# P V of the third last group ahead of the score sums of the last group, and the last V pieces issued then

## The chip, the cores and the metric

The kernel runs on one core of one Trainium2 chip. The time is device microseconds of one execution; lower is better. Each comparison takes executions of the kernel before on the same chip in the same rounds. "Group", "piece" and "span" below are meant as follows: the kernel works in 64 groups (0 to 63); the last group's V is loaded in 7 pieces; the span is the time from the first to the last instruction in a profile, about 1.8 us less than the execution's time. "P V" is the product of the exponentials of the scores (P) with V. TensorE is "warm" where its granted clock is 1.00 and "cold" where it is 0.50. Times inside a profile are microseconds from the start of its span.

## The reference, cut to what matters

```python
q = (x @ wq).reshape(B, Sq, H, Dh)                      # B=8, Sq=1, H=32, Dh=128
scores = einsum("bhqd,bhkd->bhqk", q, k_cache) * Dh**-0.5   # Sk=4096
p = softmax(scores)
o = einsum("bhqk,bhkd->bhqd", p, v_cache)
a = o.reshape(B, Sq, H * Dh) @ wo
# ... b = a small MLP of x; result g * a + (1 - g) * b
```

K and V are 512 MiB together in bf16 and each element is used once, so reading them is nearly all of the work. The MLP runs in the shadow of the loads and does not matter here.

## The kernel before

A group is four heads of one batch row: 4 MB of K and 4 MB of V. There are two K buffers and two V buffers; group g uses buffer g % 2. For each group VectorE multiplies K by q in four chunks, TensorE adds the products up in 8 matmuls per chunk ("score sum" of the chunk), VectorE reduces the rest, and after the fourth chunk comes the softmax. P V of a group is done one group later, on TensorE, in the stream of the next group's score sums.

```python
def load_v_pieces(g):                       # only for the last group, 63
    s = g % 2
    ...
        t = load("sync", dst, part, f"sVl{n}", [v_done.get(g - 2)])   # buffer is free after P V of 61

def scores(g, between):                     # mult: VectorE product and TensorE sum of a chunk
    mult(g, 0); between(0)
    mult(g, 1); between(1)
    for c in range(NCK):                    # NCK = 4
        reduce(g, c)
        if c + 2 < NCK:
            mult(g, c + 2); between(c + 2)

def between(c, g=g):
    ...
    if c == 2:
        ...
        if g == NG - 1:                     # NG - 1 = 63, NG - 3 = 61
            pv(NG - 3, 0, 1)
            evict(NG - 3)
            load_v_pieces(g)
    if c == 3:
        if 1 <= g < NG - 2:
            pv(g - 1, 0, 1)                 # the other groups: behind sum 3
            evict(g - 1)
        ...
```

K of groups 62 and 63, V of 61 and V of 62 are all issued before the last V pieces. After the last group's scores follow P V of 62, the exponentials of 63, "turned" P V of 63 (128 small matmuls, each needing its V piece), the output projection and the store. Instructions are emitted per engine in program order; in the timelines below the matmuls run in that order.

Of the kernel before, what the change touches and what calls it, by code (L numbers as in the profile page):

```python
# [23 lines left out]
NG = NHG * B  # L24
# [11 lines left out]
class Stream:  # L36
# [8 lines left out]
    def op(self, engine, fn, waits=(), dma=None):  # L45

        rec = [fn, [w for w in waits if w is not None], None, dma]
        self.ops[engine].append(rec)
        if dma is not None:
            return ("dma", *dma)  # L50
        return ("op", engine, rec)
# [33 lines left out]
def bass_gated_mix__mha_block_cached__mixer_channel_mlp__decode_kernel(  # L85
# [20 lines left out]
    def pstride(t):  # L106
        return t[tuple([slice(None)] * len(t.shape))].ap[0][0]
# [78 lines left out]
    def load(engine, dst, src, name, waits=()):  # L186
        return op(engine, lambda e: e.dma_start(dst, src), waits, dma=(nc.alloc_semaphore(name), 16))  # L187
# [24 lines left out]
    def kv_src(cache, g):  # L212
        hg, b = divmod(g, B)
        return cache[b, hg * HB:(hg + 1) * HB].rearrange("h (p t) d -> (h p) t d", p=32)
# [4 lines left out]
    def load_k(g):  # L219
        s = g % 2  # L220
        nK[s] += 1
        src = kv_src(A_k_cache, g)
        k_land[g] = op("sync", lambda e: e.dma_start(KB[s][:, :, :], src), [k_done.get(g - 2)], dma=(sK[s], 16 * nK[s]))

    def load_v(g):
        s = g % 2
        nV[s] += 1
        src = kv_src(A_v_cache, g)
        t = op("sync", lambda e: e.dma_start(VB[s][:, :, :], src), [v_done.get(g - 2)], dma=(sV[s], 16 * nV[s]))
        v_land[g] = [(t, 0, NTT)]  # L230
# [3 lines left out]
    def load_v_pieces(g):  # L234
        s = g % 2
        src = kv_src(A_v_cache, g)
        v_land[g] = []
        t0 = 0
        for n, nt in enumerate(V_LAST):
            dst, part = VB[s][:, t0:t0 + nt, :], src[:, t0:t0 + nt, :]  # L240
            t = load("sync", dst, part, f"sVl{n}", [v_done.get(g - 2)])
            v_land[g].append((t, t0, t0 + nt))
            t0 += nt
        assert t0 == NTT
# [140 lines left out]
    def softmax(g):  # L385
        s = g % 2
        t = op("vector", lambda e: e.tensor_reduce(out=mA[:, 0:1], in_=s_sb[:, s, :], axis=AX.X, op=ALU.max),  # L387
               [v_red[g, NCK - 1], c_mA])
        t = op("vector", lambda e: e.transpose(mB[:, :], mA[:, :]), [t])  # L389
        t = op("vector", lambda e: e.tensor_reduce(out=gm[:, :], in_=mB[:, :], axis=AX.X, op=ALU.max), [t])  # L390
        gmb = bass.AP(tensor=gm, offset=0, ap=[[pstride(gm), 128], [0, 32]])
        t = op("vector", lambda e: e.tensor_scalar(out=mC[:, :], in0=gmb, scalar1=-1.0, scalar2=None, op0=ALU.mult), [t])
        v_nm[g] = op("vector", lambda e: e.transpose(mD[:, s, :], mC[:, :]), [t, a_exp.get(g - 2)])  # L393
        for h in range(HB):
            q = slice(32 * h, 32 * h + 32)
            a_exp[g] = op("scalar", lambda e, h=h, q=q: e.activation(  # L396
                out=P[q, s, :, h], in_=s_sb[q, s, :], func=ACT.Exp, bias=mD[q, s, 0:1], scale=1.0),
                [v_nm[g], p_pv.get(g - 2), v_rs.get(g - 2), c_P])

    def rowsum(g):  # L400
        s = g % 2
        v_rs[g] = op("vector", lambda e: e.tensor_reduce(  # L402
            out=rs[:, s, :], in_=P[:, s, :, :].rearrange("p t h -> p h t"), axis=AX.X, op=ALU.add),
            [a_exp[g], p_z.get(g - 2)])

    def pv(g, part, parts):
        s = g % 2
        for land, t0, t1 in v_land[g]:
            t0, t1 = max(t0, part * NTT // parts), min(t1, (part + 1) * NTT // parts)
            for tq in range(t0 // TQ, t1 // TQ):  # L410
                j = tq % 4
                o = o_ps[s][32 * j:32 * j + TQ * HB, :]
                w = [land, a_exp[g], a_ev.get(g - 2), *c_ps] if tq == t0 // TQ else ()
                p_pv[g] = op("tensor", lambda e, o=o, tq=tq: e.matmul(  # L414
                    o, lhsT=P[:, s, tq * TQ:(tq + 1) * TQ, :].rearrange("p t h -> p (t h)"),
                    rhs=VB[s][:, tq * TQ:(tq + 1) * TQ, :].rearrange("p t d -> p (t d)"),
                    start=(tq < 4), stop=(tq >= NTQ - 4)), w)
        v_done[g] = p_pv[g]

    def total(g):  # L420
        p_z[g] = op("tensor", lambda e: e.matmul(  # L421
            oz_ps[:, HB:2 * HB], lhsT=ones[:, :], rhs=rs[:, g % 2, :], start=True, stop=True),
            [v_rs[g], v_norm.get(g - 1), c_ones])

    def evict(g):
        s = g % 2
        a_ev[g] = op("scalar", lambda e: e.activation(out=O_sb[:].rearrange("p t d -> p (t d)"), in_=o_ps[s][:, :],  # L427
                                                      func=ACT.Copy), [p_pv[g], p_oz.get(g - 1)])

    def gather(g):  # L430
        for tt in range(TQ):
            p_oz[g] = op("tensor", lambda e, tt=tt: e.matmul(  # L432
                oz_ps[:, 0:HB], lhsT=O_sb[:, tt, :], rhs=sel16[:, tt, :], start=(tt == 0), stop=(tt == TQ - 1)),
                [a_ev[g], v_norm.get(g - 1), c_sel16] if tt == 0 else ())

    def norm(g):
        hg, b = divmod(g, B)
        t = op("vector", lambda e: e.reciprocal(out=rz[:, :], in_=oz_ps[:, HB:2 * HB]), [p_oz[g]])  # L438
        v_norm[g] = op("vector", lambda e: e.tensor_tensor(  # L439
            out=OT_sb[:, hg * HB:(hg + 1) * HB, b], in0=oz_ps[:, 0:HB], in1=rz[:, :], op=ALU.mult), [t])  # L440
# [4 lines left out]
    def up_proj(j0, j1):  # L445
        for jt in range(j0, j1):
            for kt in range(NKF + 2):
                o, n, at = up_ps[:, jt * B:(jt + 1) * B], 128, kt * F + jt
                if kt >= NKF:
                    o, n, at = up_ps[64 * (kt - NKF):64 * (kt - NKF) + 64, jt * B:(jt + 1) * B], 64, NKF * F + jt  # L450
                w = bass.AP(tensor=RB, offset=at, ap=[[pstride(RB), 128], [NJ, n]])
                st["p_up"] = op("tensor", lambda e, w=w, o=o, kt=kt: e.matmul(  # L452
                    o, lhsT=w, rhs=yT_sb[:, kt, :], start=(kt == 0), stop=(kt >= NKF)),
                    [*ld_w1, v_yT] if jt == kt == 0 else ())
# [27 lines left out]
    def down_proj(j0, j1):  # L482
        for jt in range(j0, j1):
            st["p_down"] = quarters(hT_sb[:, jt, :], w2_sb[:, jt, :], jt == 0, jt == NJ - 1,
                                    [st["ld_w2"], st["v_h"], c_yps] if jt == 0 else ())
# [41 lines left out]
    for g in range(NG):  # L527
        if 1 <= g <= NG - 3:
            load_k(g + 1)
        if 1 <= g <= NG - 2 and g != NG - 3:  # L530
            load_v(g)

        def between(c, g=g):
            if c == 0 and 2 <= g < NG - 1:
                gather(g - 2)
            if c == 1 and g >= 1:
                rowsum(g - 1)
                if g < NG - 1:
                    if g >= 2:
                        norm(g - 2)  # L540
                    total(g - 1)
            if c == 2:
                if UP0 <= g < UP0 + UPN:
                    up_proj((g - UP0) * NJ // UPN, (g - UP0 + 1) * NJ // UPN)
                if DN0 <= g < DN0 + DNN:
                    down_proj((g - DN0) * NJ // DNN, (g - DN0 + 1) * NJ // DNN)
                if g >= AP0 and done_a[0] * B + B + 1 <= g:
                    a_proj(done_a[0])
                    done_a[0] += 1
                if g == NG - 1:  # L550
                    pv(NG - 3, 0, 1)
                    evict(NG - 3)
                    load_v_pieces(g)
            if c == 3:
                if 1 <= g < NG - 2:
                    pv(g - 1, 0, 1)
                    evict(g - 1)
                if g == NG - 1:
                    gather(NG - 3)
                if g == UP0 + UPN:  # L560
                    act_h()
                if g == DN0 + DNN:
                    b_out()

        scores(g, between)
        if g == NG - 3:
            load_k(g + 2)
            load_v(g)
        if g + 1 < NG:
            q_of(g + 1)  # L570
        if g == UP0 + UPN:
            load_w2()
        if g == DN0 + DNN:
            load_wo()
        softmax(g)
    last = NG - 1
    norm(last - 2)
    pv(last - 1, 0, 1)
# [54 lines left out]
```

## Time and profile before

| | kernel before |
|---|---|
| time, median (3 executions) | 1313.88 us (1313.2 to 1313.92) |
| span of the profile | 1313.1 us |
| mean load rate | 425 GB/s |
| last V pieces issued from | 1295.41 us |
| last piece landed | 1309.0 us |
| last reduce of group 63 | 1297.24 us |

The load stream bounds the kernel over almost the whole span. From the page of the kernel before: DMA is the busy share, in tenths, of 40 slices of the span; the line under it is what they moved in GB/s.

```profile
DMA  9999999999999999999999999999999999999996
GB/s 400 417 431 434 432 432 429 430 432 433 429 434 431 432 428 430 422 420 431 432 432 431 431 432 430 431 431 432 431 431 431 431 431 430 431 432 429 431 411 268
```

Only the last slices fall off. Among the waits of SyncE, which issues the loads, is this one (who waited, for what; us in total, times, longest):

```profile
SPq L187 <- PE psb L414: 32.7, 1, 32.7
```

L187 is the issue of the V pieces, L414 is P V. Most of such a wait costs nothing, because earlier loads keep the DMA busy. The windows view, one microsecond each (busy shares of TensorE, its weight loads, VectorE, ScalarE, GpSimd; granted clock; DMA share; GB/s), shows what this wait costs the stream:

```profile
1289.00:1290.00 1.00, 1.00 (x4) 0.32 (x3) 1.00 (x2) 0.00 (x0) 0.00 (x0) 0.50 0.23 98
...
1292.00:1293.00 1.00, 1.00 (x7) 0.45 (x5) 1.00 (x2) 0.00 (x0) 0.00 (x0) 1.00 0.16 66
1293.00:1294.00 1.00, 1.00 (x15) 0.35 (x17) 1.00 (x1) 0.00 (x0) 0.00 (x0) 1.00 0.00 0
1294.00:1295.00 1.00, 1.00 (x28) 0.40 (x16) 0.97 (x2) 0.00 (x0) 0.00 (x0) 1.00 0.00 0
1295.00:1296.00 1.00, 1.00 (x12) 0.35 (x5) 0.00 (x0) 0.58 (x1) 0.00 (x0) 1.00 0.00 0
1296.00:1297.00 1.00, 1.00 (x6) 0.53 (x5) 0.00 (x0) 0.01 (x1) 0.00 (x0) 1.00 0.85 147
```

The queue has nothing left and stands idle until the pieces are issued. A packet counts in the window in which it starts; by the packets of the trace no data move from 1294.13 to 1296.37. The stream also thins out ahead of that, to 98 GB/s in the microsecond from 1289. The timeline of TensorE, VectorE and SyncE in that stretch (start, duration, engine, line, operation, count, idle time before and its releaser):

```profile
1285.05 6.31 PE L364 MATMUL psb<-p,ident 128*128 128x512 bf16 x16 [4.16 <-DVE p L354]
1288.68 0.69 DVE L369 TENSOR_REDUCE s_sb<-psb 128x32 f32<-128x512 f32 x1 [0.89 <-PE psb L364]
1291.63 1.90 PE L364 MATMUL psb<-p,ident 128*128 128x512 bf16 x8 [0.27 <-DVE p L354]
1293.46 1.90 PE L414 MATMUL psb<-VB,P 128*16 128x512 bf16 x32
1295.30 1.90 PE L364 MATMUL psb<-p,ident 128*128 128x512 bf16 x8
1295.41 3.46 SPq L187 DMA_DIRECT2D VB<-in_A_v_cache_dram  x7
1297.24 0.69 DVE L369 TENSOR_REDUCE s_sb<-psb 128x32 f32<-128x512 f32 x1 [2.26 <-PE psb L364]
...
1307.75 1.02 PE L508 MATMUL psb<-P,VB 128*128 128x4 bf16 x24 [2.01 <-DMA VB<-in_A_v_cache_dram]
1309.03 0.37 PE L508 MATMUL psb<-P,VB 128*128 128x4 bf16 x8 [0.25 <-DMA VB<-in_A_v_cache_dram]
```

L364 with x8 is one score sum. P V of group 61 runs at 1293.46, the pieces go out when it is done, and the last turned matmuls (L508) wait for them 2 us and more. Yet V of group 61 had landed at 1284.5 (issued at 1258.92, 25.6 us to landing in the view of the DMA issues).

One more thing to see: the 16 matmuls that start at 1285.05 take 6.31 us, while later ones take 1.90 us for 8. The page's clock line and the windows view give the reason: the granted TensorE clock was 0.50 from 1283.7 to 1290.5 (the first of the windows above shows it).

### The profile page before, as it was taken

How to read it: one execution, taken by the hardware profiler on the slowest of the kernel's cores; microseconds unless marked ns; L12 is line 12 of the kernel's file. 1: busy time of each engine (PE TensorE's matmuls, PEld its weight loads, DVE VectorE, ACT ScalarE, POOL GpSimd, SP SyncE). 2: the span in 40 equal slices, each digit the busy share in tenths (PEclk: the TensorE clock that was granted, in tenths of full speed). 3: DMA queues.
4: the chain of work that ended last, by engine and by line, in shares of the span. 5: the costliest groups of instructions: out<-in, count | busy, mean ns of one | idle time of the engine just before them, and what ended most of it. 6: DMA issues, size and time to landing. Idle time of an engine off the chain costs nothing.

```text
span 1313.1 us, 12641 instructions
## 1 busy us (share of the span) xinstructions
PE 877.7 (67%) x5428; PEld 419.8 (32%) x5428; DVE 871.2 (66%) x1061; ACT 204.1 (16%) x393; POOL 2.5 (0%) x13
## 2 busy tenths in 40 slices
PE   3466877676638676646766755766676776676686
PEld 1133433343313333222332322333232333232233
DVE  4576676676747676646667676676676676776665
ACT  1201011111110110101111111111111111101101
POOL 0000000000000000000000000000000000000000
PEclk8878777968777888778868888777868777878877
DMA  9999999999999999999999999999999999999996
GB/s 400 417 431 434 432 432 429 430 432 433 429 434 431 432 428 430 422 420 431 432 432 431 431 432 430 431 431 432 431 431 431 431 431 430 431 432 429 431 411 268
DMA packets 25255, 557.77 MB, mean 425 GB/s; under 512 B 2528, under 2 KB 6640, under 8 KB 7536
## 3 DMA queue, kind: packets, MB, share of 16 engines
q1 hardware_dynamic: 24944, 556.95, 99.0%
q8 instruction: 42, 0.69, 0.2%
q14 instruction: 13, 0.11, 0.0%
q10 hardware_dynamic: 256, 0.03, 0.0%
HBM read 556.96 MB, written 0.01 MB: 424 GB/s over the span
## 4 chain that ended last, share of the span: by engine, by line
DMA 65%; DVE 18%; PE 16%; ACT 0%; issue 0%; SPq 0%
DMA KB<-in_A_k_cache_dram 64%; DVE p L354 14%; PE psb L364 13%; PE psb L432 3%; DVE s_sb L369 3%; DMA VB<-in_A_v_cache_dram 1%; PE psb L414 0%; SPq L187 0%; DVE rz L438 0%; DVE OT_sb L439 0%; ACT P L396 0%; ACT L467 0%; ACT O_sb L427 0%; PE psb L477 0%; DVE mA L387 0%
## 5 line engine op out<-in xcount | busy, mean ns | idle before, releaser
L364 PE MATMUL psb<-p,ident 128*128 128x512 bf16 x2048 | 645.5, 473 | 413.9 <-DVE p L354 413.9
L354 DVE TENSOR_TENSOR p<-KB,q_bc 128x4096 bf16<-128x4096 bf16 x256 | 579.5, 2285 | 181.7 <-DMA KB<-in_A_k_cache_dram 178.6
L364 PEld LDWEIGHTS psb<-p,ident 128*128 128x128 bf16 x2048 | 225.2, 120 | 725.2 <-DVE p L354 447.7
L369 DVE TENSOR_REDUCE s_sb<-psb 128x32 f32<-128x512 f32 x256 | 175.6, 686 | 103.9 <-PE psb L364 103.7
L427 ACT ACTIVATE O_sb<-psb 128x512 f32<-128x512 f32 x63 | 37.6, 597 | 1037.9 <-PE psb L414 1037.9
L396 ACT ACTIVATE P<-s_sb,mD 32x128 bf16<-32x128 f32 x256 | 147.0, 574 | 10.6 <-DVE mD L393 6.7
L414 PE MATMUL psb<-VB,P 128*16 128x512 bf16 x2016 | 119.9, 379 | 0.0
L432 PEld LDWEIGHTS psb<-sel,O_sb 128*128 128x128 f32 x504 | 101.9, 280 | 21.3 <-issue 16.3
L438 DVE RECIPROCAL rz<-psb 128x4 f32<-128x4 f32 x63 | 11.5, 182 | 125.6 <-PE psb L432 125.6
L432 PE MATMUL psb<-sel,O_sb 128*128 128x4 f32 x504 | 88.2, 298 | 0.0
L414 PEld LDWEIGHTS psb<-VB,P 128*16 128x16 bf16 x2016 | 44.7, 89 | 69.9 <-issue 26.3
L402 DVE TENSOR_REDUCE rs<-P 128x4 f32<-128x512 bf16 x64 | 43.5, 679 | 2.1 <-ACT P L396 2.1
L421 PEld LDWEIGHTS psb<-rs,ones 128*128 128x128 f32 x128 | 31.3, 246 | 15.8 <-issue 8.6
L348 ACT ACTIVATE q_bc<-psb 128x128 bf16<-128x128 f32 x64 | 17.4, 271 | 32.4 <-PE psb L346 32.4
L421 PE MATMUL psb<-rs,ones 128*128 128x4 f32 x128 | 21.2, 236 | 0.0
L452 PEld LDWEIGHTS psb<-yT_sb,RB 128*128 128x128 bf16 (+1 forms) x216 | 19.4, 165 | 3.4
L452 PE MATMUL psb<-yT_sb,RB 128*128 128x8 bf16 (+1 forms) x216 | 19.8, 227 | 0.0
L387 DVE TENSOR_REDUCE mA<-s_sb 128x1 f32<-128x128 f32 x64 | 18.3, 286 | 2.2
L389 DVE STREAM_TRANSPOSE mB<-mA 128x32 f32<-128x32 f32 x64 | 13.6, 213 | 2.2
L393 DVE STREAM_TRANSPOSE mD<-mC 128x32 f32<-128x32 f32 x64 | 13.6, 212 | 2.2
L346 PEld LDWEIGHTS psb<-Q,Sel 128*128 128x128 bf16 x64 | 6.1, 96 | 27.4 <-issue 27.2
L346 PE MATMUL psb<-Q,Sel 128*128 128x128 bf16 x64 | 14.7, 230 | 0.0
(63 smaller groups left out, 86.5 us busy)
## 6 DMA issues: line engine op xcount, KB each, us to landing
KB<-in_A_k_cache_dram SPq DMA_DIRECT2D x64, 4096.0 KB, 26.0
VB<-in_A_v_cache_dram SPq DMA_DIRECT2D x63, 4096.0 KB, 31.8
RB<-in_B_w_dram SPq DMA_DIRECT2D x1, 5184.0 KB, 43.8
RB<-in_B_w_dram SPq DMA_DIRECT2D x1, 4608.0 KB, 35.8
RB<-in_A_wo_dram SPq DMA_DIRECT2D x1, 4608.0 KB, 43.9
RB<-in_A_wq_dram SPq DMA_DIRECT2D x1, 4096.0 KB, 12.6
VB<-in_A_v_cache_dram SPq DMA_DIRECT2D x2, 1024.0 KB, 5.7
VB<-in_A_v_cache_dram SPq DMA_DIRECT2D x3, 512.0 KB, 8.4
```

Source lines behind the costliest of these rows:

```text
L346: t = op("tensor", lambda e: e.matmul(qb_ps[:, 0:DH], lhsT=Sel[:, b, :], rhs=Q4[:, hg * DH:(hg + 1) * DH], start=True, stop=True), [a_Q[hg ...
L354: v_mult[g, c] = op("vector", lambda e: e.tensor_tensor(out=p1[:, par, :, :], in0=KB[s][:, c * CT:(c + 1) * CT, :], in1=qb, op=ALU.mult), ...
L364: p_sum[g, c] = op("tensor", lambda e, r=r, n=n: e.matmul(tr_ps[par][:, :], lhsT=ident[:, :], rhs=r, start=(n == 0), stop=(n == NCH - 1)), w)
L369: v_red[g, c] = op("vector", lambda e: e.tensor_reduce(out=s_sb[:, s, c * CT:(c + 1) * CT], in_=tr_ps[par][:, :].rearrange("p (t c) -> p t ...
L387: t = op("vector", lambda e: e.tensor_reduce(out=mA[:, 0:1], in_=s_sb[:, s, :], axis=AX.X, op=ALU.max), [v_red[g, NCK - 1], c_mA])
L396: a_exp[g] = op("scalar", lambda e, h=h, q=q: e.activation(out=P[q, s, :, h], in_=s_sb[q, s, :], func=ACT.Exp, bias=mD[q, s, 0:1], scale=1.0),
L402: v_rs[g] = op("vector", lambda e: e.tensor_reduce(out=rs[:, s, :], in_=P[:, s, :, :].rearrange("p t h -> p h t"), axis=AX.X, op=ALU.add), ...
L414: p_pv[g] = op("tensor", lambda e, o=o, tq=tq: e.matmul(o, lhsT=P[:, s, tq * TQ:(tq + 1) * TQ, :].rearrange("p t h -> p (t h)"), rhs=VB[s] ...
L421: p_z[g] = op("tensor", lambda e: e.matmul(oz_ps[:, HB:2 * HB], lhsT=ones[:, :], rhs=rs[:, g % 2, :], start=True, stop=True), [v_rs[g], v_ ...
L427: a_ev[g] = op("scalar", lambda e: e.activation(out=O_sb[:].rearrange("p t d -> p (t d)"), in_=o_ps[s][:, :], func=ACT.Copy), [p_pv[g], p_ ...
L432: p_oz[g] = op("tensor", lambda e, tt=tt: e.matmul(oz_ps[:, 0:HB], lhsT=O_sb[:, tt, :], rhs=sel16[:, tt, :], start=(tt == 0), stop=(tt == ...
L452: st["p_up"] = op("tensor", lambda e, w=w, o=o, kt=kt: e.matmul(o, lhsT=w, rhs=yT_sb[:, kt, :], start=(kt == 0), stop=(kt >= NKF)), [*ld_w ...
```

## The change

P V of group 61 moves ahead of all score sums of group 63, so that the buffer is free and the last V pieces are issued as soon as V of 61 is there. Nothing else changes. The order of the other engines' instructions stays as it was; only TensorE's order changes.

```diff
                     done_a[0] += 1
-                if g == NG - 1:
-                    pv(NG - 3, 0, 1)
-                    evict(NG - 3)
-                    load_v_pieces(g)
             if c == 3:
@@
         softmax(g)
+        if g == NG - 2:
+            pv(g - 1, 0, 1)
+            evict(g - 1)
+            load_v_pieces(g + 1)
     last = NG - 1
```

## The prediction

> **What bounds the kernel now.** Over the span it is the load stream: 425 GB/s mean, 99% of the queue's time (page, parts 2 and 3). The change touches only the last 30 us. There the SyncE waits and the timeline show one hole: the last V pieces (group 63) are issued at 1295.4 us, after a 32.7 us wait for P V of group 61, although V of group 62 landed at 1294.6 (issue 1262.4 + 32.2). One-microsecond windows show 66, 0, 0, 0, 147 GB/s from 1292 to 1297. The last piece lands at 1309.0, and the chain of waits ends with it; norm, output projection and store follow to 1313.1.
>
> P V of group 61 could run earlier: its V lands at 1284.5 (issue 1258.92 + 25.6). It stands behind the score sums of chunks 0 to 2 of group 63, which wait for VectorE's products.
>
> **What the change moves.** Nothing is added or removed; 32 P V matmuls go from between chunk sums 2 and 3 to ahead of chunk sum 0. TensorE will wait for V of group 61 (1284.5), run P V, and release the pieces at about 1287.5 to 1288.2, 7 us sooner. The hole closes; the last piece should land at about 1304.5 (estimate: 1294.6 plus 4 MB at 430 GB/s, 9.8 us).
>
> **What that costs.** The score sums of group 63 become the limit. Today chunk sum 0 starts at 1285.05. With P V ahead it starts near 1288, because TensorE runs at half clock there: it idled from 1280.9, and the granted clock is 0.50 from 1283.7 to 1290.5. A chunk sum takes 3.6 us cold and 1.90 warm; P V takes 1.90 warm, so I estimate 3.6 cold. The clock changes only at steps of 3.413 us, and rose only after a step with at least 2.68 us of score or P V matmuls (never after 2.60). The Trainium skill, "TensorE: Matmul & The Clock Gate", Part 1, states this free-running window; the trace agrees. So cold time after 1284.5 is 2.7 to 6.1 us by the phase, and chunk sum 0 ends at 1289.7 to 1291.4 (now 1288.66). Reduce, product, reduce, product, last sum take another 7.65 us: the last reduce starts at 1297.3 to 1299.1. Today it starts at 1297.24, of which 0.9 us is P V ahead of the last chunk sum; that comes back. Net delay of the softmax 0.1 to 1.8 us, mean about 1.
>
> **Sum.** Without DMA waits the tail now would run turned P V from 1301.7 to 1305.74 (with gather, total), then 32 more matmuls, 1.1 us: 1306.9. With the delay: 1307.0 to 1308.7, against 1309.4 now. Of 5 us earlier data, 0.7 to 2.4 us reach the end.
>
> **Prediction:** 1312.5 us (before 1313.88), range 1311.3 to 1314.0. Chances: faster by over 2% 0.005, within 2% 0.99, slower by over 2% 0.005.
>
> **What would show it.** Pieces issued near 1288; no empty windows around 1294; last piece landed before 1305.5; P V of 61 starts near 1284.5 at clock 0.50 and takes over 3 us; first reduce of group 63 starts 1 to 2.8 us after 1288.68, the last 0 to 1.8 us after 1297.24; the last turned P V matmuls wait for no DMA.
>
> **What would make it wrong.** P V may not count as activity for the clock (16 of 128 columns): then the sums stay cold, the delay is near 3 us and the change loses 0.5 us. V of 61 or the pieces may land later than estimated.

## More of the kernel before

The profiled execution took 1314.88 us.

## The result, and the profile after

| | before | changed |
|---|---|---|
| time, median (4 executions each) | 1313.9 us (1313.2 to 1314.78) | 1312.42 us (1311.7 to 1314.29) |
| span of the profile | 1313.1 us | 1310.0 us |
| last V pieces issued from | 1295.41 us | 1287.68 us |
| last piece landed | 1309.0 us | 1304.4 us |
| first / last reduce of group 63 | 1288.68 / 1297.24 us | 1289.50 / 1297.18 us |

The ratio is 0.9991, 95% interval 0.9973 to 1.0008: not even certainly faster in this first comparison. Ratios in this text are the mean time of one kernel's fast runs over that of the other's in the same rounds, so not quite the ratio of the medians quoted.

The changed kernel ran in three later calls too, five executions each, on three different chips. Of all 19 executions the median is 1311.9 us (1310.14 to 1314.29); of the 31 of the kernel before that ran beside them it is 1313.6 us (1312.66 to 1314.87). The medians differ by 1.7 us. The changed kernel spreads over 4.2 us, the kernel before over 2.2 us; the spread has to be explained as well as the gain.

The page of the changed kernel, the same two lines; the last slice moves 295 GB/s instead of 268:

```profile
DMA  9999999999999999999999999999999999999997
GB/s 401 418 432 431 432 431 431 432 432 432 432 429 431 430 430 432 425 417 432 432 431 432 430 432 431 432 430 432 431 429 431 430 432 431 431 432 432 431 418 295
```

The wait of SyncE after the change:

```profile
SPq L187 <- PE psb L414: 26.5, 1, 26.5
```

The same stretch in the windows view after the change, with two earlier lines; the stream no longer stops, though it still thins out where V of 62 ends (180 GB/s in the microsecond from 1289):

```profile
1285.00:1286.00 1.00, 1.00 (x16) 0.34 (x12) 1.00 (x2) 0.00 (x0) 0.00 (x0) 0.50 1.06 459
...
1289.00:1290.00 1.00, 1.00 (x7) 0.45 (x5) 0.50 (x1) 0.00 (x0) 0.00 (x0) 1.00 0.62 180
...
1292.00:1293.00 1.00, 0.55 (x3) 0.31 (x4) 1.00 (x3) 0.00 (x0) 0.00 (x0) 1.00 0.75 311
1293.00:1294.00 1.00, 1.00 (x7) 0.39 (x4) 1.00 (x1) 0.00 (x0) 0.00 (x0) 1.00 0.94 385
1294.00:1295.00 1.00, 0.35 (x2) 0.00 (x0) 1.00 (x1) 0.00 (x0) 0.00 (x0) 1.00 0.97 410
1295.00:1296.00 1.00, 0.76 (x4) 0.40 (x5) 0.79 (x2) 0.00 (x0) 0.00 (x0) 1.00 1.01 393
```

And the timeline:

```profile
1284.28 3.35 PE L414 MATMUL psb<-VB,P 128*16 128x512 bf16 x32 [4.93 <-DMA VB<-in_A_v_cache_dram]
1287.56 3.63 PE L364 MATMUL psb<-p,ident 128*128 128x512 bf16 x16
1287.68 4.04 SPq L187 DMA_DIRECT2D VB<-in_A_v_cache_dram  x7
1289.50 0.69 DVE L369 TENSOR_REDUCE s_sb<-psb 128x32 f32<-128x512 f32 x1 [3.25 <-PE psb L364]
...
1297.18 0.69 DVE L369 TENSOR_REDUCE s_sb<-psb 128x32 f32<-128x512 f32 x1 [1.40 <-PE psb L364]
...
1304.44 1.85 PE L508 MATMUL psb<-P,VB 128*128 128x4 bf16 x64
```

P V now waits for the landing of V of 61 and starts at 1284.28. It takes 3.35 us instead of 1.90, because the clock is at 0.50 from 1283.83 to 1287.25. The pieces go out 7.7 us sooner. At the end the 64 last turned matmuls run in one stretch and wait for no load. The chain of waits (start, duration, what) has changed its nature; before it ended with a load,

```profile
1298.43 10.55 DMA VB<-in_A_v_cache_dram
1309.03 0.39 PE psb L508 x8
```

and now its last load is V of group 61, and compute follows from there to the end:

```profile
1257.41 26.83 DMA VB<-in_A_v_cache_dram
1284.24 0.04 issue
1284.28 3.35 PE psb L414 x32
1287.63 1.85 PE psb L364 x8
1289.47 0.02 issue
1289.50 0.69 DVE s_sb L369
...
1304.58 1.72 PE psb L508 x64
```

So 7.7 us of earlier issue became 4.6 us of earlier landing (the queue had to finish V of 62 first, and its own end is slow: 219 and 195 GB/s in the two microseconds from 1301), and of these 3.1 us reached the end of this profile (1313.1 to 1310.0). This compares a slow execution of the kernel before (1314.88 us) with a fast one of the changed kernel (1311.82 us); the medians of all executions differ by 1.7 us.

### The profile page after: what moved, and what is told of

The parts are those of the page before. It is cut to its first block, busy times and chain, and to the rows that moved or that the text cites. A ratio compares the mean times of both kernels' runs of the same rounds, so it can differ in the third digit from the quotient of the medians.

```text
span 1310.0 us, 12641 instructions
## 1 busy us (share of the span) xinstructions
PE 870.3 (66%) x5428; PEld 416.0 (32%) x5428; DVE 870.8 (66%) x1061; ACT 204.1 (16%) x393; POOL 2.5 (0%) x13
## 4 chain that ended last, share of the span: by engine, by line
DMA 66%; DVE 17%; PE 16%; issue 0%; ACT 0%; SPq 0%
DMA KB<-in_A_k_cache_dram 64%; DVE p L354 14%; PE psb L364 12%; PE psb L432 3%; DVE s_sb L369 3%; DMA VB<-in_A_v_cache_dram 2%; PE psb L414 0%; PE psb L508 0%; DVE rz L438 0%; DVE OT_sb L439 0%; ACT P L396 0%; ACT L467 0%; SPq L187 0%; SPq L223 0%; PE psb L477 0%
## 5 line engine op out<-in xcount | busy, mean ns | idle before, releaser
L364 PE MATMUL psb<-p,ident 128*128 128x512 bf16 x2048 | 638.9, 469 | 415.7 <-DVE p L354 415.7
L432 PEld LDWEIGHTS psb<-sel,O_sb 128*128 128x128 f32 x504 | 99.7, 274 | 21.0 <-issue 16.2
L432 PE MATMUL psb<-sel,O_sb 128*128 128x4 f32 x504 | 86.3, 294 | 0.0
```

The source lines that it names most:

```text
L364: p_sum[g, c] = op("tensor", lambda e, r=r, n=n: e.matmul(tr_ps[par][:, :], lhsT=ident[:, :], rhs=r, start=(n == 0), stop=(n == NCH - 1)), w)
L432: p_oz[g] = op("tensor", lambda e, tt=tt: e.matmul(oz_ps[:, 0:HB], lhsT=O_sb[:, tt, :], rhs=sel16[:, tt, :], start=(tt == 0), stop=(tt == ...
```

## The experiments

Theory: two limits end this kernel. One is the landing of the last piece, set by when the pieces are issued. The other is the chain of score sums, softmax and turned P V of group 63, which P V of 61 now heads. The first limit moved away; the second decides, and its length depends on whether TensorE's clock is at half rate there. The clock changes only at steps of 3.413 us whose phase differs between executions, which gives the spread. Rivals: the moved 1.9 us on TensorE bring the gain, not the loads; or the spread comes from the landing of V of 61, not from the clock.

All eleven runs gave correct results. "chip 10" and so on are names of chips; times are compared within one call.

### First call (chip 10): the kernel before 1313.99 us, 9 executions, 1313.18 to 1314.87

**The changed kernel again.** No edit.

> The changed kernel again, unaltered, for a second look at its spread. Theory (the clock's phase decides whether P V of group 61 and the first score sum of group 63 run cold): executions spread over about 1311.5 to 1314.5 us, median near 1312.5; if the profiled one is a slow one, the granted clock stays 0.50 until 6 us after P V starts and the first reduce of group 63 comes about 1.8 us later than in the trace at hand (1289.5). Rival (V of group 61 lands at different times, the clock does not matter): in a slow trace P V starts over 1 us later than 1284.3, with the first chunk sum at 1.9 us.

Measured: 1311.54 us (1310.14 to 1313.96), ratio 0.9982 (0.9969 to 0.9994). The traced execution was the fastest one, with a span of 1308.3 us. Its timeline, to be read beside that of the first profile of the changed kernel:

```profile
1283.89 1.90 PE L414 MATMUL psb<-VB,P 128*16 128x512 bf16 x32 [3.65 <-DMA VB<-in_A_v_cache_dram]
1285.73 3.63 PE L364 MATMUL psb<-p,ident 128*128 128x512 bf16 x16
1287.66 0.69 DVE L369 TENSOR_REDUCE s_sb<-psb 128x32 f32<-128x512 f32 x1 [0.53 <-PE psb L364]
```

P V started only 0.4 us sooner than in the first profile, but at full clock: it took 1.90 us, and the first reduce came 1.8 us sooner. The prediction had taken it for granted that the clock is low there. It is not always: the 3.413 us step of the clock from 1281.96 on held 1.48 us of P V, and the clock did not fall after it. Two of the five executions (1310.14 and 1310.38) lie below the 1311.5 that was expected.

**Only the order.** TensorE's order as changed; the pieces wait also for VectorE's last product, so that they are issued as late as before.

```diff
-            t = load("sync", dst, part, f"sVl{n}", [v_done.get(g - 2)])
+            t = load("sync", dst, part, f"sVl{n}", [v_done.get(g - 2), hold])
@@ c == 3, g == NG - 1
+                    load_v_pieces(g, v_mult[g, 3])
@@ after softmax(NG - 2)
-            load_v_pieces(g + 1)
```

> TensorE's order as in the changed kernel, but the last V pieces also wait for VectorE's last product of group 63 (about 1295.2 us), so they are issued about when the kernel before issued them. Theory (the earlier issue brings the gain, the earlier P V alone only costs): last piece lands near 1309, the last turned P V waits for it, time 1313.3 to 1314.3, no gain over the kernel before. Rival (it is the 0.9 us that P V took ahead of the last chunk sum that brings the gain): 1312.5, like the changed kernel.

Measured: 1314.87 us (1314.75 to 1315.01), ratio 1.0007 (0.9995 to 1.002). Pieces issued from 1295.06, the last turned matmuls wait 2.2 us for a load again. All of the gain is gone; the new order by itself brings nothing, and it may cost a little. The time is 0.6 us above the range that was expected; the hold ends at the late edge of when the kernel before issues its pieces. The spread is only 0.26 us, less than the clock theory suggests for a hold that follows the score sums; one trace doesn't tell why.

**Only the early load.** TensorE's order as before; the last V pieces go to the buffer of K of group 62, which is free at about 1278.5, and need not wait for P V of 61.

```diff
-            dst, part = VB[s][:, t0:t0 + nt, :], src[:, t0:t0 + nt, :]
-            t = load("sync", dst, part, f"sVl{n}", [v_done.get(g - 2)])
+            dst, part = KB[1 - s][:, t0:t0 + nt, :], src[:, t0:t0 + nt, :]
+            t = load("sync", dst, part, f"sVl{n}", [k_done[g - 1]])
@@ pv_turned
-  lhsT=VB[s][:, t, :]
+  lhsT=KB[1 - s][:, t, :]
@@ c == 2, g == NG - 1
-                    load_v_pieces(g)
@@ after softmax(g)
+        if g == NG - 2:
+            load_v_pieces(g + 1)
```

> TensorE's order as in the kernel before, but the last V pieces go into the buffer of K of group 62, which is free at about 1279, so they need not wait for P V of group 61 and follow V of group 62 without a hole. Theory: the last piece lands near 1304, the last turned P V waits for no DMA, and the tail of sums and exponentials ends the kernel: 2.0 to 2.6 us less than the kernel before, 1311.3 to 1311.9, with a spread under 1.5 us. Rival (the tail is bound by something that follows the loads, for instance VectorE slowed by the denser stream): under 1 us gained.

Measured: 1310.69 us (1310.38 to 1311.63), ratio 0.9977 (0.9965 to 0.999). Pieces issued from 1278.46; no turned matmul waits for a load:

```profile
1303.19 1.85 PE L508 MATMUL psb<-P,KB 128*128 128x4 bf16 x64
```

The load alone gives the whole gain and somewhat more than expected: 3.1 us by the means (1310.96 against 1314.03), while the changed kernel has 2.5 us in the same call. The two experiments together settle where the gain comes from: from the issue time, not from the order.

Issuing still sooner than the changed kernel does, though, did not make the last piece land sooner: 1304.42 for an issue from 1278.46, and 1304.39 in the first profile of the changed kernel for one from 1287.68. In both the stream ends slowly; here it moved 252, 229 and 227 GB/s in the three microseconds from 1299:

```profile
1301.00:1302.00 1.00, 1.00 (x19) 1.00 (x16) 0.00 (x0) 0.00 (x0) 0.00 (x0) 1.00 0.58 227
```

So what this version has over the changed kernel is not an earlier landing. In these two profiles its last reduce comes sooner (1295.80 against 1297.18), because no P V waits for a load ahead of the score sums; no run tests that alone.

**Clock kept up.** The changed kernel, with 14 filler matmuls into an unused PSUM bank ahead of P V of 61.

```diff
+    def warm(n):
+        for i in range(n):
+            op("tensor", lambda e: e.matmul(up_ps[:, :], lhsT=ident[:, :], rhs=Q4[:, 0:512], start=True, stop=True),
+               [st["v_hb"]] if i == 0 else ())
@@ after softmax(NG - 2)
+            warm(14)
             pv(g - 1, 0, 1)
```

> The changed kernel with 14 extra 128x512 matmuls into an unused PSUM bank ahead of P V of group 61, in TensorE's idle time from 1279.4 to 1284.3, which keep the granted clock at 1.00. Theory (the cold clock is the cost): P V takes 1.9 instead of 3.35 us or more, the first reduce of group 63 starts near 1288.1, the last reduce near 1295.7; every execution is like that, spread under 1 us; time 1310.3 to 1311.3. Rival (cold clock is of no account): 1312.5 with the spread of the changed kernel.

Measured: 1311.96 us (1310.3 to 1312.56), ratio 0.9981 (0.9967 to 0.9995). By the means this is 1311.65 us against 1311.53 us of the changed kernel in the same call: no gain. The spread is 2.3 us, where under 1 was expected. The local effect is as expected: P V took 1.90 us, and the first reduce came 3.78 us after its start. The time is not: two things were left out. V of 61 landed at 1284.90 in this trace, and the tail had a second clock effect. The landing is no chance: in the nine traces without a filler V of 61 lands 9.71 to 9.73 us after K of 63, in the four with one 10.17 to 10.57 us after it. So the filler goes with a delay of 0.4 to 0.9 us just where P V waits for that load; what in it does so is not shown. As to the tail, the gather of group 62 (L432, 8 fp32 matmuls) ran cold:

```profile
1301.67 1.85 PE L432 MATMUL psb<-sel,O_sb 128*128 128x4 f32 x8
```

In the first profile of the changed kernel it took 1.03 us. That is 0.8 us on the chain, from a clock drop at 1301.68.

### Second call (chip 9): the kernel before 1313.04 us, 9 executions, 1312.78 to 1313.74

**The changed kernel a third time.**

> The changed kernel a third time, beside the other runs of this call. Clock theory, now with both limits read from the traces (the clock rises after a 3.413 us step with at least 2.63 us of score, P V or filler matmuls, and falls after one with under about 1.5 us): executions between 1310 and 1314.3 us, median near 1311.8. In the traced one, the start of the first reduce of group 63 minus the start of P V is 3.8 us if P V and sum are all warm, 5.2 if the clock rises about 2.8 us after P V starts, up to 6.9 if it rises 6 us after, and the end moves by the same.

Measured: 1312.03 us (1311.69 to 1313.83), ratio 0.9995 (0.9983 to 1.0008). (The expectation puts the limit for a fall of the clock at about 1.5 us; that is too high, see the last section.) Here the traced execution was the slowest, span 1312.0 us:

```profile
1284.09 3.59 PE L414 MATMUL psb<-VB,P 128*16 128x512 bf16 x32 [3.63 <-DMA VB<-in_A_v_cache_dram]
1287.62 4.53 PE L364 MATMUL psb<-p,ident 128*128 128x512 bf16 x16
1290.46 0.69 DVE L369 TENSOR_REDUCE s_sb<-psb 128x32 f32<-128x512 f32 x1 [3.11 <-PE psb L364]
...
1303.43 1.85 PE L432 MATMUL psb<-sel,O_sb 128*128 128x4 f32 x8
```

P V started sooner than in the first profile, so a late load is not what made it slow. The clock stayed at 0.50 until 1289.49, through P V and most of the first sum, and the gather was cold too. The four traces of the changed kernel, with the fourth from the third call:

| trace | P V starts | clock 0.50 until | first reduce, after P V's start | last reduce | gather | span |
|---|---|---|---|---|---|---|
| second | 1283.89 | (stayed 1.00) | 3.77 us | 1295.35 | 1.03 us | 1308.3 |
| first | 1284.28 | 1287.25 | 5.22 us | 1297.18 | 1.03 us | 1310.0 |
| fourth | 1284.43 | 1288.17 | 5.41 us | 1297.53 | 1.03 us | 1310.3 |
| third | 1284.09 | 1289.49 | 6.37 us | 1298.14 | 1.85 us | 1312.0 |

In these four the end follows the clock, not the landing of V of 61, which differs by 0.5 us over the four.

**Clock kept up in the kernel before.** The same 14 fillers at the same place, with TensorE's order of the kernel before (no other edit).

> TensorE's order of the kernel before, with 14 filler matmuls in TensorE's idle time ahead of the first score sum of group 63. Clock theory: the first sum takes 1.9 us in every execution, the pieces are issued near 1293.9, and the time is at the low edge of the spread of the kernel before, 1313.0 to 1313.6, spread under 0.7 us. Rival (the spread of the kernel before comes from the loads): median as before, 1313.9, spread as before, 1.7 us.

Measured: 1313.42 us (1312.52 to 1313.99), ratio 1.0002 (0.9989 to 1.0014). This missed: neither the median nor the spread fell (1313.04 and 1.0 us in the nine executions of the kernel before in this call; 1313.42 and 1.5 us here). The trace starts the products of group 63 at 1282.74, as the profile of the kernel before does, so those two can be laid side by side. The first reduce is at 1287.70 instead of 1288.68, the pieces are issued from 1294.42 instead of 1295.41, and the span is 1312.2 instead of 1313.1. So the filler gave 1 us there, but VectorE was the next limit, busy until 1287.7 with other work. It doesn't remove what happens ahead of it, in group 62, either: in the traces of the changed kernel the products of 63 start anywhere from 1281.20 to 1282.31. The expected spread of under 0.7 us had left that out. That this made the spread is likely, but no run tests it.

**P V between sums 1 and 2.** Half way: the pieces still wait for P V of 61.

```diff
             if c == 1 and g >= 1:
+                if g == NG - 1:
+                    pv(NG - 3, 0, 1)
+                    evict(NG - 3)
+                    load_v_pieces(g)
                 rowsum(g - 1)
@@ the four lines under c == 2 are gone, as in the change
```

> P V of group 61 between score sums 1 and 2 of group 63, and the last pieces issued then: halfway between the two kernels. Theory (two limits: the landing of the last piece, 13.6 us after the issue, and the chain of score sums): pieces issued at 1292 to 1293.3, about 2 us sooner than before; the last reduce of group 63 no later than in the kernel before; time 1311.5 to 1312.5, spread under 1.7 us. Rival (any move of P V ahead costs the score sums what the loads gain): near 1313.5.

Measured: 1311.38 us (1310.47 to 1311.51), ratio 0.9984 (0.9972 to 0.9997): 0.65 us less than the changed kernel in the same call by the medians, 1.4 us by the means (1311.08 against 1312.47), with half of its spread. Pieces issued from 1293.0; the last reduce at 1296.55, no later than in the kernel before. TensorE runs P V for the most part in time in which it waits for VectorE's product anyway: from the first to the last reduce of group 63 it takes 8.12 us in this trace, 8.56 in the kernel before and 7.68 in the changed one. In this call a smaller advance of the load served better; it cost the score sums nothing against the kernel before.

**Early load, P V between sums 1 and 2, and the filler.** The edits of "only the early load", of the last experiment (without its load) and of the filler together.

> The candidate for a version that beats both: the last V pieces go into the buffer of K of group 62 (issued near 1278.5), P V of group 61 stands between score sums 1 and 2, where TensorE waits for VectorE anyway, and 14 filler matmuls keep the clock up ahead of sum 0. Theory: the last reduce starts near 1294.8, the turned P V begins near 1299.3, the last piece (near 1303.5 to 1304) and the tail (near 1304) end together; 1309.3 to 1310.3, spread under 1 us. Rival (the landing of the pieces or the tail has a floor that the clock does not move): 1310.7, like the version with the other buffer alone.

Measured: 1310.39 us (1310.17 to 1310.67), ratio 0.9979 (0.9966 to 0.9993). The spread is 0.5 us. The median is 0.1 us above the expected range: the last reduce (1294.09) was as early as expected, but the last piece landed at 1304.54. The turned matmuls wait for the last pieces again, for 0.4 us and more:

```profile
1304.59 0.37 PE L508 MATMUL psb<-P,KB 128*128 128x4 bf16 x8 [0.40 <-DMA KB<-in_A_v_cache_dram]
```

The stream is the limit once more, and executions agree. It never stops now, but it ends slowly: 268, 234, 233 and 227 GB/s in the four microseconds from 1298.

### Third call (chip 11): the kernel before 1313.61 us, 9 executions, 1312.66 to 1314.86

**Two fillers.** The changed kernel with 14 fillers ahead of P V of 61 and 6 ahead of the turned P V.

```diff
     rowsum(last)
+    warm(6)
     pv_turned(last, (0,))
```

> The changed kernel with 14 filler matmuls ahead of P V of group 61, and 6 more in TensorE's wait for the last exponentials, so that the gather of group 62, which took 1.85 us cold and 1.03 warm in the traces at hand, is warm too. Theory (two clock terms, one ahead of the sums and one in the tail): from the last reduce of group 63 to the end 12.8 to 13.0 us in the trace (14.4 with the first filler alone), time 1310.0 to 1311.3, spread under 1.3 us, which is what the landing of V of group 61 leaves. Rival (the fillers leave something else open): as with the first filler alone, 1312.0, spread 2.3 us.

Measured: 1310.56 us (1310.24 to 1311.73), ratio 0.9979 (0.9966 to 0.9991); the changed kernel in the same call has 1312.02 us. The gather was warm:

```profile
1301.85 1.03 PE L432 MATMUL psb<-sel,O_sb 128*128 128x4 f32 x8
```

From the last reduce (1296.58) to the end it was 13.4 us, not 12.8 to 13.0; the store accounts for it, which took 3.0 us from its issue to the end of the span against 2.4 us in the first profile of the changed kernel. The spread is 1.5 us where under 1.3 was expected; V of 61 landed at 1285.1 in the traced one, which is the slowest. So keeping the clock up in both places is worth 1.5 us by the medians of this call and 1.1 us by the means; what is left is the landing of V of 61, which the filler itself goes with (above), and the store. The spread did not shrink here: the changed kernel's own is 0.6 us in this call.

**Early load and P V between sums 1 and 2, without filler.**

> The best version without the filler matmuls: V of the last group into the buffer of K of group 62, P V of group 61 between score sums 1 and 2. Theory: with the last piece landing near 1304 the score sums have about 1 us of room, so the filler is worth 0 to 0.7 us: 1310.3 to 1311.2. Rival (the filler carries the gain of that version): 1311.5 or more.

Measured: 1310.35 us (1310.27 to 1310.68), ratio 0.9975 (0.9961 to 0.9989). The fillers carry nothing here, and this is the version with the largest gain: 3.2 us under the kernel before by the means (1310.40 against 1313.64), 1.6 us under the changed kernel, and with a spread of 0.4 us. It never ran beside the load-only version, which gained 3.1 us in its own call, so that moving P V adds anything to the early load is not shown. Its score sums ran at half clock for a while as well (16 matmuls in 5.31 us), but there was room for it.

```profile
1283.51 5.31 PE L364 MATMUL psb<-p,ident 128*128 128x512 bf16 x16 [4.15 <-DVE p L354]
...
1304.43 0.38 PE L508 MATMUL psb<-P,KB 128*128 128x4 bf16 x8 [0.26 <-DMA KB<-in_A_v_cache_dram]
```

**The changed kernel a fourth time.**

> The changed kernel beside these two on the same chip: 1310 to 1314.3 us again, median 1311.5 to 1312.4; the traced execution once more has the interval from the start of P V to the first reduce of group 63 between 3.8 and 6.9 us, and its end moves with it.

Measured: 1312.02 us (1311.73 to 1312.37), ratio 0.9987 (0.9975 to 1.0). The five executions lie within 0.6 us, so the wide spread is not seen in every call. The trace is the fourth line of the table above: 5.41 us from P V's start to the first reduce.

## Why the prediction was right or wrong

- **The time.** 1312.5 us predicted, 1312.42 us measured. That it is so close is partly luck: the four executions spread over 2.6 us, the median of all 19 is 1311.94 us, and the gain was worked out on the profile of a slow execution (1314.88 us) but subtracted from the median of others (1313.88 us). The range of 1311.3 to 1314.0 held 16 of all 19 executions; two were faster (1310.14 and 1310.38) and one slower (1314.29).
- **The hole in the stream, and that it closes: right.** Pieces issued at 1287.68 (1287.5 to 1288.2 predicted), last landing 1304.4 (1304.5), no empty windows. That this is the whole source of the gain is shown by the two halves: early load alone, 3.1 us gained; order alone, nothing.
- **The score sums become the limit: right.** The chain of waits of the changed kernel runs through P V, sums, reduces, exponentials; no turned matmul waits for a load. The 0.9 us of P V ahead of the last sum came back as said (first to last reduce 7.68 instead of 8.56 us). But two of the named signs missed in the first profile: the first reduce came 0.82 us after 1288.68 (1 to 2.8 said), the last 0.06 us before 1297.24 (0 to 1.8 after it said).
- **P V cold, 3.6 us: right in three traces of four** (3.31 to 3.59 us), wrong in the second (1.90 us).
- **"TensorE runs at half clock there": the step that failed.** It took the one trace of the kernel before, a slow execution with two cold steps, for every execution. TensorE idles 3.6 to 4.9 us ahead of P V, about one step of the clock, so whether one step is idle enough for a drop depends on the phase. "Cold time 2.7 to 6.1 us" is the range when it has dropped; in the second trace it was 0. The last reduce therefore came 1.9 us sooner to 0.9 us later than the 1297.24 of the kernel before, where 0.1 to 1.8 us later had been predicted. Of the four traced executions the fastest is the one in which the step fails; for the untraced ones this is not shown.
- **The threshold for the rise, "at least 2.68 us": right in kind, slightly off.** Over all thirteen traces the limit lies at 2.63 us (last section).
- **Left out: the tail.** The gather can run cold, 1.85 instead of 1.03 us. In the slowest traced execution of the changed kernel that is 0.8 us on the chain.
- **"P V may not count as activity for the clock": it counts.** In the first profile the clock rose at 1287.25, at the end of a step whose 2.97 us of work was P V alone.

What stays open: why the chips differ (the kernel before has medians of 1313.99, 1313.04 and 1313.61 us on the three, and the changed kernel gained 2.5, 0.6 and 1.6 us by the means), what moves the landing of V of 61 between 1283.85 and 1284.48 without a filler, why it is later still with one, and the small spread of the order-only version.

## What to carry to other kernels

When a load waits for a buffer, look first for another buffer that is free by then; here the K buffer of the group before gave the early issue without touching TensorE's order, and more of the time than the move of P V did (3.1 us against 2.5 us in the same call). If work must move to free a buffer, move it to where its engine waits anyway, not to the head of the chain that becomes the next limit. And where an idle TensorE sits ahead of that chain, count with both clock rates, and look at more than one execution before you take one of them for granted, and see where the profiled one lies among the timed ones. Filler matmuls are no free remedy: here they went with a later load.

## What the Trainium skill lacked or had wrong

- "TensorE: Matmul & The Clock Gate", Part 1, states a free-running window of 3413 ns and that the clock falls after an idle window and rises after a busy one. The traces agree with the window: the clock changed only at multiples of 3.413 us. How busy is busy is not given. In the thirteen traces (from 110 us to 1296 us of the span, about 4,500 steps) every rise followed a step with at least 2.63 us of bf16 score, P V and filler matmuls (767 of them; 1,029 cold steps below that, up to 2.63 us, brought none), and every fall a step with at most 1.31 us of them (762; the least without a fall had 1.35 us). That is 77% and about 39% of the step. A step need not be idle for a fall.
- The same page tells to avoid idle gaps of over about 3 us, and to keep TensorE busy. For matmuls that are no transposes, no page says that some kinds do not keep it up; here some did not. A step with 2.46 us of gather and turned P V matmuls (fp32 or 4 columns wide) was followed by a fall, at 1304.16 in the kernel before; and steps with TensorE busy for all 3.41 us, but only 2.05 us of it with score sums and the rest with the fp32 gather, brought no rise. P V, 16 of 128 columns, did count: a step with 2.97 us of it alone was followed by a rise, at 1287.25 in the changed kernel.
- "DMA: Bandwidth & Descriptors", "Anatomy of one DMA", gives about 2 us of fixed cost (for loads issued by GpSimd; these are SyncE's), most of it the receipt after the last byte. The kernel before shows less of it: the last data packet of V of group 62 ended at 1294.13 and the load landed at 1294.55, 0.4 us later; from the issue of the first V piece (1295.41) to its first packet (1296.37) it was 1.0 us. No page says how much the end of a deep queue frays: there the stream fell to 98 GB/s in the microsecond from 1289, and to 66 in the one from 1292, with the mean busy share of the 16 engines between 0.16 and 0.68 in those four. Where the pieces follow early, the end of the stream does the same (busy share 0.58 in the line from 1301 of the load-only version).
- No page has the effect of the fillers on a load: V of group 61 landed 9.71 to 9.73 us after K of 63 without them, 10.17 to 10.57 us with them.
